# A scan followed by a feed-forward block: order of the first scan, one visit for the outputs of four sequences, accumulator sums on VectorE

## The chip, the cores and the metric

One core of one Trainium2 chip. The metric is the device time of one execution in microseconds (us). All times quoted are of fast runs. The granted TensorE clock is 0.996 to 1.0 in every profiled run.

## The reference

```python
# 4 sequences, 8 heads, 768 positions, head_dim 32, d_state 16, fp32; a is a decay in 0.85..0.95
for c in chunks:                                   # the reference uses chunks of 32 positions
    L = exp(cum_i - cum_j) * causal                # decay between positions of a chunk
    y = (C @ B^T * L) @ x + (C @ state) * exp(cum)
    state = exp(sum(log a)) * state + sum_j decay_j * B_j x_j
x = y as 3072 tokens x 256
h = x @ w_in                                       # 256 -> 2048
out = (h * cos(h)) @ w_out                         # 2048 -> 256
```

## The kernel before

The scan runs in six chunks of 128 positions. While the feed-forward block of chunk c runs in 16 steps, the scan of chunk c+1 is woven into it. A step n: TensorE makes `hp` (128 columns of d_ff times two, for two sequences), ScalarE rounds to whole turns (`k`), VectorE subtracts (`w`), ScalarE takes the cosine, VectorE multiplies (`gT`). Two steps later TensorE multiplies by w_out; from chunk 1 on by a scheme with seven products instead of eight, which needs differences `gd` of gT (GpSimd) and, at the end of each half chunk, sums of seven accumulators. In the first chunk the weights are also rounded for the matrix unit: ScalarE takes `mag` and `last` out of the `words`, GpSimd clips, VectorE joins (two instructions), GpSimd adds (this is called a join below).

The parts that the change touches:

```python
def turn(b, tag=None):                             # transposes of B and C of one sequence, chunk 0
    tp = pair("tp")[:, 0] if tag is None else bank([P, 4 * P], "tp", tag)
    ...
def intra(b):                                      # g = C B^T of 8 heads, then m = g * lam on VectorE
    g = [pair("g") for _ in range(2)]              # a pair is two PSUM banks
    ...
# the first chunk's scan
fill(warm, 2); fill(warm[:, 0:2])                  # warm products: their result is not used
spread_a(0, "h"); turn(0); spread_a(1, "h"); spread_a(2, "o"); spread_a(3, "h")
for b in range(NB): decays0(b)                     # four scans on VectorE
turn(1, "h"); cross(0, "o"); intra(0); turn(2, "h"); cross(2, "o"); intra(1); finish(0, "o")
grade("in", 0, n=2); intra(2); turn(3, "h"); finish(1, "o", 1)
...                                                # decays cut and written to DRAM
join("in", 0); finish(2, "o"); intra(3); grade("in", 1); join("in", 1)

# in step n of the feed-forward block
first(n)                                           # hp, k, w
gate(n)                                            # sine
if not early and n in piece: join(*piece[n])
gated(n)                                           # gT, and gd on GpSimd
second(n - LAG)                                    # products with w_out; after the last of a half: sums
for c, u in pairs(n - 1): intra2(c, u); masked(c, 2 * u)
for c, u in pairs(n - 2): masked(c, 2 * u + 1)
for c, u in pairs(n - 3): finish2(c, u)            # y of two sequences, their part of the state
for c, b, t in halves_at(n): decays(c, b, t)       # half a scan on VectorE, 1.2 to 2.1 us
# TURN = (NF - 5, NF + 3): the pairs' transposes in steps 11 and 19, so two y visits a chunk
# sums of accumulators: four G.tensor_tensor of 128x256 or 128x128
```

Of the kernel before, what the change touches and what calls it, by code (L numbers as in the profile page):

```python
# [25 lines left out]
def kernel(  # L26
# [210 lines left out]
    unit0 = const.tile([P, H, W], FP32, name="unit0")  # L237
# [36 lines left out]
    a0s = const.tile([P, 2, H, W], FP32, name="a0s")  # L274
# [6 lines left out]
    tos = const.tile([P, H, W], FP32, name="tos")  # L281
# [32 lines left out]
    def cross(b, tag):  # L314

        ps = bank([P, H, W], "l_ps", tag)
        PE.matmul(ps, lhsT=fros[:, b:b + 2].rearrange("p b j -> p (b j)"), rhs=tos,
                  start=True, stop=True)
        for t in range(2):
            ACT.copy(out=lam[0, b + t][0:W, 1], in_=ps[t * W:(t + 1) * W])  # L320
            weigh(0, b + t)
# [31 lines left out]
    def turn(b, tag=None):  # L353

        bc = raw[0][0]
        tp = (pair("tp")[:, 0] if tag is None else bank([P, 4 * P], "tp", tag)
              ).rearrange("p (k i) -> p k i", k=4)
        for k in range(2):
            PE.transpose(tp[:, k], bc[:, k, heads(b)].rearrange("p h n -> p (h n)"), ident)

        cT = scan.tile([P, 2, P], FP32, tag="cT", name="cT")
        for t in range(2):
            ACT.activation(cT[:, t], tp[:, 1], AF.Copy, scale=slot[:, t:t + 1])
        bT = scan.tile([P, P], FP32, tag="bT", name="bT")
        ACT.copy(out=bT, in_=tp[:, 0])
        part[0, b] = (bT, cT)

    def intra(b):
# [6 lines left out]
        l = lam.pop((0, b))  # L375
        m = scan.tile([P, 2, H, W], FP32, tag="m", name="m")
# [5 lines left out]
        part[0, b] = m  # L382

# [15 lines left out]
    def turn2(c, u):  # L399
# [12 lines left out]
        rT = scan.tile([P, 2, P], FP32, tag="rT", bufs=1, name="rT")  # L412
# [13 lines left out]
    def masked(c, b):  # L426
# [4 lines left out]
        m = scan.tile([P, H, P], FP32, tag="m", name="m")  # L431
# [7 lines left out]
    def finish2(c, u):  # L439
        (_, ms, rT), xr = part.pop((c, u)), raw[c][1]  # L440
# [3 lines left out]
        for s in range(2):  # L444
            for q in range(4):
                r, p = slice(32 * q, 32 * q + 32), 64 * (q % 2)
                PE.matmul(y[p:p + 64, q // 2, s * P:(s + 1) * P],  # L447
                          lhsT=state[c - 1, u][r, s].rearrange("p t d -> p (t d)"),
                          rhs=rT[r, s], start=(s == 0), stop=False, tile_position=(32 * q, p),
                          skip_group_check=True)  # L450
        for s in range(2):
            for h in range(H):
                q, t = h % 4, h // 4
                PE.matmul(y[32 * q:32 * q + 32, t, s * P:(s + 1) * P], lhsT=xr[:, 2 * u + s, h],  # L454
                          rhs=ms[s][:, h], start=False, stop=True, tile_position=(0, 32 * q),
                          skip_group_check=True)
        if u == 0:
            yT[c] = two.tile([P, 2, TB], FP32, tag="yT", name="yT")
        ACT.copy(out=yT[c][:, :, 2 * u * P:(2 * u + 2) * P], in_=y[:, :, 0:2 * P])
        if c < NC - 1:  # L460
            s_ps = pair("s_ps")[:, 0, 0:4 * D].rearrange("p (s d) -> p s d", s=2)
            for s in range(2):
                sum_up(c, 2 * u + s, s_ps[:, s])
            carry(c, u, s_ps)
# [37 lines left out]
    def first(n):  # L502
# [6 lines left out]
        for e in range(2):  # L509
            fs = slice((2 * j + e) * P, (2 * j + e + 1) * P)  # L510
            for k in range(KT):
                PE.matmul(to_[:, e], lhsT=w_in[:, k, fs], rhs=y[:, k, u],  # L512
                          start=(k == 0), stop=(k == KT - 1), skip_group_check=True)

# [66 lines left out]
    def seven(n):  # L581
# [38 lines left out]
        for dst, a_, b_ in ((sum_[:, 0:2], ps[:, 1:3], ps[:, 0:1]),  # L620
# [3 lines left out]
            G.tensor_tensor(out=dst, in0=a_, in1=b_.to_broadcast([P, dst.shape[1], P]), op=ALU.add)  # L624
# [34 lines left out]
    fill(warm[:, 0:2])  # L659
    spread_a(0, "h")  # L660
    turn(0)
    spread_a(1, "h")
    spread_a(2, "o")
    spread_a(3, "h")
    for b in range(NB):
        decays0(b)
    turn(1, "h")
    cross(0, "o")
    intra(0)
    turn(2, "h")  # L670
    cross(2, "o")
    intra(1)
    finish(0, "o")
    grade("in", 0, n=2)
    intra(2)
    turn(3, "h")
    finish(1, "o", 1)
# [6 lines left out]
    for dst, src in ((a_cut, cut), (a_all, la)):  # L684
# [3 lines left out]
    join("in", 0)  # L688
    finish(2, "o")
    intra(3)  # L690
    grade("in", 1)
    join("in", 1)
# [8 lines left out]
    TURN = (NF - 5, NF + 3)  # L701

    halves_of = {u: [(t - 4 + i, 2 * u + i // 2, i % 2) for i in range(4)]
                 for u, t in enumerate(TURN)}
    ahead = {1: {0: [(4, 0, 0), (6, 0, 1), (8, 1, 0), (9, 1, 1)]}}
# [3 lines left out]
    def first_scan():  # L709

        finish(3, "o")
# [16 lines left out]
    def pairs(n):  # L728

        at = [(1 + (n - t) // NF, u) for u, t in enumerate(TURN) if (n - t) % NF == 0]  # L730
        return [(c, u) for c, u in at if 0 < c < NC]

    def halves_at(n):
        return [(c, b, t) for c in range(1, NC) for u in range(2)
                for m, b, t in ahead.get(c, {}).get(u, halves_of[u]) if m + (c - 1) * NF == n]

    EARLY = 3
    rest_of_loads()
    for n in range(NC * NF + LAG):
        c, f = divmod(n, NF)  # L740
        early = n < EARLY
        if n < NC * NF:
            if f == 0 and c > 0:
                load(c + 2)
            first(n)
            if n == 0:
# [10 lines left out]
            if not early and n in piece:  # L757
                join(*piece[n])
            gated(n)
            if early and n in piece:  # L760
# [10 lines left out]
        for c, u in pairs(n - 2):  # L771
            masked(c, 2 * u + 1)
        for c, u in pairs(n - 3):
            finish2(c, u)
            if u == 1:
                raw.pop(c)
        for c, b, t in halves_at(n):
            decays(c, b, t)
            if t == 1:
                load_a(c + 1, (b,))  # L780
# [34 lines left out]
```

## Time and profile before

| | before |
|---|---|
| time, median of 4 (386.46 of the 3 runs that were known at the prediction) | 386.79 us |
| span of the profiled run | 384.9 us |
| first hp / second hp / first o product | 18.80 / 22.15 / 26.55 us |
| first o to the last matmul | 354.27 us |
| busy: PE, DVE, ACT, POOL | 98, 69, 45, 64% |

The third and fourth rows are read from TensorE's timeline; they cut the span into the front, in which TensorE waits, and the rest, in which it is nearly at its floor. The lines are in the prediction.

### The profile page before, as it was taken

What the parts mean: (1) busy time and instruction counts of PE and PEld (TensorE: products, weight loads), DVE (VectorE), ACT (ScalarE), POOL (GpSimd) and SP (SyncE); (2) the same over time, 40 slices, a digit from 0 to 9 for tenths busy, and PEclk for the clock granted to TensorE, in tenths of its full rate; (3) what the DMA queues carried; (4) which work ended last, traced back from release to release, by engine and by line L of the source; (5) the groups of instructions that cost most, each with busy time, mean ns of one, the idle gap of its engine ahead of it and who ended that gap; (6) DMA issues with size and microseconds to landing.
All of it is one profiled execution on the core that took longest, in us unless ns stands there. A gap on an engine that the chain in (4) does not pass through costs nothing.

```text
span 384.9 us, 7726 instructions
## 1 busy us (share of the span) xinstructions
PE 378.3 (98%) x2982; PEld 331.2 (86%) x2982; DVE 265.9 (69%) x395; ACT 172.9 (45%) x303; POOL 245.4 (64%) x366
## 2 busy tenths in 40 slices
PE   8999999999999999999999999999999999999996
PEld 3578887888899899899899899899899989989995
DVE  7879999678667658657657757756765865863443
ACT  3878566534334334335334434434433433433441
POOL 5757665458859549648648837855955855853751
PEclk9999999999999999999999999999999999999999
DMA  7989899975002951301791301201210000010001
GB/s 83 270 235 266 249 230 137 181 96 151 2 0 63 148 52 57 96 2 54 127 81 55 97 2 56 81 17 43 68 43 1 21 10 0 2 27 3 7 22 27
DMA packets 106371, 30.42 MB, mean 79 GB/s; under 512 B 75520, under 2 KB 102240, under 8 KB 106336
## 3 DMA queue, kind: packets, MB, share of 16 engines
q1 hardware_dynamic: 106176, 29.81, 38.9%
q8 instruction: 23, 0.38, 0.5%
q10 hardware_dynamic: 160, 0.13, 0.1%
q14 instruction: 12, 0.10, 0.1%
HBM read 26.59 MB, written 3.34 MB: 78 GB/s over the span
## 4 chain that ended last, share of the span: by engine, by line
PE 82%; DVE 7%; POOL 3%; ACT 2%; issue 2%; DMA 2%; SPq 1%; ACTq 0%
PE hp L512 37%; PE o L609 32%; PE g L422 3%; PE y L454 3%; DVE mag L209 2%; DVE w L518 2%; DMA xr<-in_x_dram 2%; PE y L447 2%; DVE lam L344 2%; PE o L571 1%; DVE gT L528 1%; PE warm L101 1%; ACT w L523 1%; PE a_ps L298 1%; PE tp L405 1%
## 5 line engine op out<-in xcount | busy, mean ns | idle before, releaser
L512 PE MATMUL hp<-yT,w_in 128*128 128x256 f32 x768 | 184.4, 383 | 0.6 <-POOL w_in L217 0.3
L512 PEld LDWEIGHTS hp<-yT,w_in 128*128 128x128 f32 x768 | 139.2, 190 | 22.7 <-issue 4.5
L553 POOL TENSOR_TENSOR gd<-gT 128x256 f32<-128x256 f32 x79 | 71.9, 911 | 89.5 <-DVE gT L528 86.2
L528 DVE TENSOR_TENSOR gT<-hp,w 128x512 f32<-128x512 f32 x96 | 66.3, 691 | 69.9 <-ACT w L523 60.1
L523 ACT ACTIVATE w<-w,quarter 128x512 f32<-128x512 f32 x96 | 69.3, 722 | 97.2 <-DVE w L518 97.2
L516 ACT ACTIVATE k<-hp 128x512 int32<-128x512 f32 x96 | 57.1, 595 | 90.8 <-PE hp L512 90.7
L518 DVE SCALAR_TENSOR_TENSOR w<-hp,k 128x512 f32<-128x512 f32 x96 | 65.4, 681 | 36.7 <-ACT k L516 36.4
L609 PE MATMUL o<-words,gd 128*128 128x128 f32 x474 | 67.0, 277 | 0.6 <-POOL gd L555 0.6
L609 PEld LDWEIGHTS o<-words,gd 128*128 128x128 f32 x474 | 59.3, 192 | 2.4 <-POOL gd L555 2.2
L344 DVE TENSOR_TENSOR_SCAN lam<-arow,unit 128x512 f32<-128x512 f32 x40 | 55.7, 1394 | 0.0
L609 PEld LDWEIGHTS o<-w_out,gT 128*128 128x128 f32 x316 | 46.9, 191 | 3.6
L609 PE MATMUL o<-w_out,gT 128*128 128x128 f32 x316 | 48.0, 274 | 0.0
L555 POOL TENSOR_TENSOR gd<-gT,gd 128x128 f32<-128x128 f32 x79 | 43.1, 546 | 6.2
L556 POOL TENSOR_TENSOR gd<-gT,gd 128x128 f32<-128x128 f32 x79 | 35.9, 455 | 6.2
L571 PE MATMUL o<-w_out,gT 128*128 128x256 f32 x128 | 30.3, 380 | 0.4 <-POOL w_out L217 0.4
L609 PE MATMUL o<-w_out,gd 128*128 128x128 f32 x158 | 30.6, 275 | 0.0
L609 PE MATMUL o<-words,gT 128*128 128x128 f32 x158 | 30.5, 275 | 0.0
L571 PEld LDWEIGHTS o<-w_out,gT 128*128 128x128 f32 x128 | 24.2, 190 | 4.0 <-POOL w_out L217 0.8
L435 DVE TENSOR_TENSOR m<-g,lam 128x512 f32<-128x512 f32 x40 | 25.6, 681 | 0.0
L624 POOL TENSOR_TENSOR sum<-ps,sum 128x256 f32<-128x256 f32 (+1 forms) x27 | 24.2, 909 | 1.4
L609 PEld LDWEIGHTS o<-w_out,gd 128*128 128x128 f32 x158 | 24.0, 192 | 0.0
L609 PEld LDWEIGHTS o<-words,gT 128*128 128x128 f32 x158 | 24.0, 192 | 0.0
(91 smaller groups left out, 293.9 us busy)
## 6 DMA issues: line engine op xcount, KB each, us to landing
arow<-a_cut SPq DMA_DIRECT2D x20, 512.0 KB
words<-in_moe_w_in_dram SPq DMA_DIRECT2D x8, 512.0 KB
words<-in_moe_w_out_dram SPq DMA_DIRECT2D x8, 512.0 KB
out_dram<-sum SPq DMA_DIRECT2D x18, 128.0 KB
xr<-in_x_dram SPq DMA_DIRECT2D x4, 512.0 KB
along<-a_all SPq DMA_DIRECT2D x20, 64.0 KB
xr<-in_x_dram SPq DMA_DIRECT2D x8, 128.0 KB
bc<-in_B_dram SPq DMA_DIRECT2D x4, 256.0 KB
```

Of the source, the lines that this page charges most:

```text
L344: V.tensor_tensor_scan(out=lam[c, b][:, hs].rearrange("p h i -> p (h i)"), data0=rows_.rearrange("p h i -> p (h i)"), data1=unit.rearrange ...
L435: V.tensor_tensor(out=of[0], in0=g[q][:, :, s * 2 * P:(s + 1) * 2 * P], in1=of[1], op=ALU.mult)
L512: PE.matmul(to_[:, e], lhsT=w_in[:, k, fs], rhs=y[:, k, u], start=(k == 0), stop=(k == KT - 1), skip_group_check=True)
L516: ACT.activation(k, hp[n], AF.Copy, bias=0.25, scale=INV_2PI)
L518: V.scalar_tensor_tensor(out=w, in0=hp[n], scalar=INV_2PI, in1=k, op0=ALU.mult, op1=ALU.subtract)
L523: ACT.activation(cos, cos, AF.Sin, bias=quarter, scale=TWO_PI)
L528: V.tensor_tensor(out=gT[n], in0=hp.pop(n), in1=cos, op=ALU.mult)
L553: G.tensor_tensor(out=d[:, 0:2], in0=g[:, 1:2].to_broadcast([P, 2, P]), in1=g[:, 3::-3], op=ALU.subtract)
L555: G.tensor_tensor(out=d[:, 2], in0=g[:, 0], in1=d[:, 0], op=ALU.subtract)
L556: G.tensor_tensor(out=d[:, 3], in0=g[:, 2], in1=d[:, 2], op=ALU.subtract)
L571: PE.matmul(o[c, u][:, t], lhsT=g[:, 2 * e + t], rhs=w_out[:, 2 * j + e], start=(j == e == t == 0), stop=(j == NJ - 1 and e == 1), skip_gr ...
L609: PE.matmul(at[q], lhsT=a_[q], rhs=w[q], start=(j == 0 and q in starts), stop=(j == NJ - 1), skip_group_check=True)
```

## The change

Its intent: let the first hp, which needs sequences 0 and 1 only, start earlier; enter the small-tile products of y once instead of twice per chunk; relieve GpSimd; and fill VectorE's wait for the sine. The diff, cut to its core:

```diff
-    fill(warm[:, 0:2])
-    ... four scans, then turn, cross, intra of 0 to 3 in turn
+    spread_a(0, "h"); turn(0, ...); spread_a(1, "h"); decays0(0); decays0(1)
+    cross(0, "o"); intra(0); spread_a(2, "o"); turn(1, ...); spread_a(3, "h"); decays0(2); intra(1)
+    grade("in", 0, n=2); finish(0, "o", 1); finish(1, "o", 1); join("in", 0); decays0(3)
+    turn(2, bank([P, 2 * P], "tp", "h")); cross(2, "o")
+    turn(3, intra(2)[0][:, 0, 2 * P:4 * P])       # the fourth's transposes beside the third's g
...
+    first(0, go_on=False); intra(3); turned(0)    # start(): step 0 is taken out of the loop
+    rest = grade(*piece[0], later=True); finish(2, "o"); ...; finish(3, "o"); gate(0)
+    ...; join("in", 1); gated(0); join(*piece[0])
...
+    at_once = (0, 1), {0: 7, 1: 11}, 14           # chunks 2 to 5: transposes in steps 7 and 11, one visit in 14
+    late = [((0,), {0: 11}, ..., 14), ((1,), {1: NF + 2}, ..., NF + 5)]        # chunk 1: two visits
...
+            behind = [masked(c, 2 * u + 1) for pairs(n - 2)] + [halved(...) for halves_at(n)]
+            if n not in piece and behind:
+                behind.pop(0)()                   # ahead of gT
             gated(n)
+            for do in behind: do()
...
-            G.tensor_tensor(out=dst, in0=a_, in1=b_..., op=ALU.add)     # sums of accumulators
+            V.tensor_tensor(out=dst, in0=a_, in1=b_..., op=ALU.add)
```

Three constants moved into the rotating buffers of m, which grew from two to four.

More of the change, by code (lines that the diff above doesn't have):

```diff
@@ L235 @@
     G.tensor_copy(out=unit, in_=ident.unsqueeze(1).to_broadcast([P, HH, P]))
-    unit0 = const.tile([P, H, W], FP32, name="unit0")
+    both = scan.tile([P, 2, H, W], FP32, tag="m", bufs=4, name="both")
+    unit0, tos = both[:, 0], both[:, 1]
     for t in range(2):
@@ L271 @@
                     axis=mybir.AxisListType.XY, op=ALU.add)
-    a0s = const.tile([P, 2, H, W], FP32, name="a0s")
+    a0s = scan.tile([P, 2, H, W], FP32, tag="m", bufs=4, name="a0s")
     halves = a0z.rearrange("p (t i) -> p t i", t=2)
@@ L280 @@
                         in1=mine[:, HH:H].unsqueeze(2).to_broadcast([P, HH, W]), op=ALU.mult)
-    tos = const.tile([P, H, W], FP32, name="tos")
     G.tensor_tensor(out=tos, in0=to.unsqueeze(1).to_broadcast([P, H, W]),
@@ L320, in cross @@
             ACT.copy(out=lam[0, b + t][0:W, 1], in_=ps[t * W:(t + 1) * W])
-            weigh(0, b + t)
     def weigh(c, b):
@@ L351, in decays, with turn @@
         weigh(c, b)
-    def turn(b, tag=None):
+    def turn(b, tp):
         bc = raw[0][0]
-        tp = (pair("tp")[:, 0] if tag is None else bank([P, 4 * P], "tp", tag)
-              ).rearrange("p (k i) -> p k i", k=4)
+        tp = tp.rearrange("p (k i) -> p k i", k=2)
         for k in range(2):
@@ L374, in intra @@
                       rhs=cT[r].rearrange("p t (s i) -> p s t i", s=2), start=True, stop=True)
-        l = lam.pop((0, b))
-        m = scan.tile([P, 2, H, W], FP32, tag="m", name="m")
+        l = lam[0, b]
+        m = scan.tile([P, 2, H, W], FP32, tag="m", bufs=4, name="m")
         for q in range(2):
@@ L382, in intra @@
         part[0, b] = m
+        return g
     def finish(b, tag, fills=0):
@@ L411, in turn2 @@
             ACT.activation(cT[:, :, t], tp[:, :, 1], AF.Copy, scale=slot[:, t:t + 1])
-        rT = scan.tile([P, 2, P], FP32, tag="rT", bufs=1, name="rT")
+        rT = scan.tile([P, 2, P], FP32, tag="rT", name="rT")
         V.tensor_tensor(out=rT, in0=tp[:, :, 1], in1=reach[c, u], op=ALU.mult)
@@ L430, in masked @@
         l = lam.pop((c, b))
-        m = scan.tile([P, H, P], FP32, tag="m", name="m")
+        m = scan.tile([P, H, P], FP32, tag="m", bufs=4, name="m")
         for q in range(2):
@@ L437, in masked, with finish2 @@
         ms.append(m)
-    def finish2(c, u):
-        (_, ms, rT), xr = part.pop((c, u)), raw[c][1]
+    def finish2(c, us):
+        xr = raw[c][1]
+        parts = [(2 * u + s, part[c, u][1][s], part[c, u][2][:, s]) for u in us for s in range(2)]
         y = pair("y")
-        for s in range(2):
+        for i, (b, _, rT) in enumerate(parts):
             for q in range(4):
                 r, p = slice(32 * q, 32 * q + 32), 64 * (q % 2)
-                PE.matmul(y[p:p + 64, q // 2, s * P:(s + 1) * P],
-                          lhsT=state[c - 1, u][r, s].rearrange("p t d -> p (t d)"),
-                          rhs=rT[r, s], start=(s == 0), stop=False, tile_position=(32 * q, p),
+                PE.matmul(y[p:p + 64, q // 2, i * P:(i + 1) * P],
+                          lhsT=state[c - 1, b // 2][r, b % 2].rearrange("p t d -> p (t d)"),
+                          rhs=rT[r], start=(i == 0), stop=False, tile_position=(32 * q, p),
@@ L450, in finish2 @@
                           skip_group_check=True)
-        for s in range(2):
+        for i, (b, m, _) in enumerate(parts):
             for h in range(H):
                 q, t = h % 4, h // 4
-                PE.matmul(y[32 * q:32 * q + 32, t, s * P:(s + 1) * P], lhsT=xr[:, 2 * u + s, h],
-                          rhs=ms[s][:, h], start=False, stop=True, tile_position=(0, 32 * q),
+                PE.matmul(y[32 * q:32 * q + 32, t, i * P:(i + 1) * P], lhsT=xr[:, b, h],
+                          rhs=m[:, h], start=False, stop=True, tile_position=(0, 32 * q),
@@ L456, in finish2 @@
                           skip_group_check=True)
-        if u == 0:
-            yT[c] = two.tile([P, 2, TB], FP32, tag="yT", name="yT")
-        ACT.copy(out=yT[c][:, :, 2 * u * P:(2 * u + 2) * P], in_=y[:, :, 0:2 * P])
+        s_ps = pair("s_ps")[:, 0].rearrange("p (u s d) -> p u s d", u=2, s=2)
+        for i, u in enumerate(us):
+            del part[c, u]
+            if u == 0:
+                yT[c] = two.tile([P, 2, TB], FP32, tag="yT", name="yT")
+            ACT.copy(out=yT[c][:, :, 2 * u * P:(2 * u + 2) * P],
+                     in_=y[:, :, 2 * i * P:(2 * i + 2) * P])
+            for s in range(2 if c < NC - 1 else 0):
+                sum_up(c, 2 * u + s, s_ps[:, u, s, 0:2 * D])
@@ L460, in finish2 @@
         if c < NC - 1:
-            s_ps = pair("s_ps")[:, 0, 0:4 * D].rearrange("p (s d) -> p s d", s=2)
-            for s in range(2):
-                sum_up(c, 2 * u + s, s_ps[:, s])
-            carry(c, u, s_ps)
+            for u in us:
+                carry(c, u, s_ps[:, u, :, 0:2 * D])
     def sum_up(c, b, s_ps):
@@ L500, in turn_of, with first @@
         return (f % 2, f // 2) if c == 0 else divmod(f, NJ)
-    def first(n):
+    def first(n, go_on=True):
         c, f = divmod(n, NF)
@@ L513, in first, with turned @@
                           start=(k == 0), stop=(k == KT - 1), skip_group_check=True)
+        if go_on:
+            turned(n)
+    def turned(n):
         k = ffn.tile([P, TB], I32, tag="k", name="k")
@@ L623, in seven @@
                             (sum_[:, 2:3], ps[:, 6:7], sum_[:, 6:7])):
-            G.tensor_tensor(out=dst, in0=a_, in1=b_.to_broadcast([P, dst.shape[1], P]), op=ALU.add)
+            V.tensor_tensor(out=dst, in0=a_, in1=b_.to_broadcast([P, dst.shape[1], P]), op=ALU.add)
         for s in range(2):
@@ L658 @@
     fill(warm, 2)
-    fill(warm[:, 0:2])
     spread_a(0, "h")
-    turn(0)
+    turn(0, pair("tp")[:, 0, 0:2 * P])
     spread_a(1, "h")
-    spread_a(2, "o")
-    spread_a(3, "h")
-    for b in range(NB):
-        decays0(b)
-    turn(1, "h")
+    decays0(0)
+    decays0(1)
     cross(0, "o")
     intra(0)
-    turn(2, "h")
-    cross(2, "o")
-    intra(1)
-    finish(0, "o")
-    grade("in", 0, n=2)
-    intra(2)
-    turn(3, "h")
-    finish(1, "o", 1)
+    spread_a(2, "o")
+    turn(1, bank([P, 2 * P], "tp", "h"))
+    spread_a(3, "h")
+    decays0(2)
+    intra(1)
+    grade("in", 0, n=2)
+    finish(0, "o", 1)
+    finish(1, "o", 1)
+    join("in", 0)
+    decays0(3)
+    turn(2, bank([P, 2 * P], "tp", "h"))
+    cross(2, "o")
+    turn(3, intra(2)[0][:, 0, 2 * P:4 * P])
     la = const.tile([RB, NU, P], FP32, name="la")
@@ L686 @@
             out=dst.rearrange("(u b) h (c p) -> (b h c) u p", u=NU, p=P), in_=src)
-    join("in", 0)
-    finish(2, "o")
-    intra(3)
-    grade("in", 1)
-    join("in", 1)
+    later = grade("in", 1, later=True)
     piece = {n: ("in", (n + 3) // 2) if n % 2 else ("out", n // 2) for n in range(NF)}
@@ L698 @@
                  NF + 1: [(0, hind), (1, hind)], NF + 3: [(2, hind), (3, hind)]}
-    TURN = (NF - 5, NF + 3)
-    halves_of = {u: [(t - 4 + i, 2 * u + i // 2, i % 2) for i in range(4)]
-                 for u, t in enumerate(TURN)}
-    ahead = {1: {0: [(4, 0, 0), (6, 0, 1), (8, 1, 0), (9, 1, 1)]}}
+    late = [((0,), {0: 11}, [(4, 0, 0), (6, 0, 1), (8, 1, 0), (9, 1, 1)], 14),
+            ((1,), {1: NF + 2}, [(NF - 2 + i, 2 + i // 2, i % 2) for i in range(4)], NF + 5)]
+    at_once = (0, 1), {0: 7, 1: 11}, 14
+    halves_of = {2: [(2, 0, 0), (3, 0, 1), (5, 1, 0), (6, 1, 1), (7, 2, 0), (8, 2, 1), (10, 3, 0),
+                     (11, 3, 1)]}
+    each = [(i - 1, i // 2, i % 2) for i in range(2 * NB)]
+    plan = [(c, NF * (c - 1), *v) for c in range(1, NC) for v in (
+        late if c == 1 else [(*at_once[:2], halves_of.get(c, each), at_once[2])])]
     sums = {}
     def first_scan():
-        finish(3, "o")
         for u in range(2):
@@ L728, in pairs, with halved, ends, start @@
     def pairs(n):
-        at = [(1 + (n - t) // NF, u) for u, t in enumerate(TURN) if (n - t) % NF == 0]
-        return [(c, u) for c, u in at if 0 < c < NC]
+        return [(c, u) for c, at, _, turn_at, _, _ in plan for u in turn_at
+                if at + turn_at[u] == n]
     def halves_at(n):
-        return [(c, b, t) for c in range(1, NC) for u in range(2)
-                for m, b, t in ahead.get(c, {}).get(u, halves_of[u]) if m + (c - 1) * NF == n]
+        return [(c, *h) for c, at, _, _, halves_of, _ in plan for m, *h in halves_of if at + m == n]
+    def halved(c, b, t):
+        decays(c, b, t)
+        if t == 1:
+            load_a(c + 1, (b,))
+    def ends(n):
+        return [(c, us) for c, at, us, _, _, end in plan if at + end == n]
+    def start():
+        first(0, go_on=False)
+        intra(3)
+        turned(0)
+        rest = grade(*piece[0], later=True)
+        finish(2, "o")
+        for b in range(NB):
+            weigh(0, b)
+            del lam[0, b]
+        finish(3, "o")
+        gate(0)
+        for do in (later, rest):
+            if do:
+                do()
+        join("in", 1)
+        gated(0)
+        join(*piece[0])
     EARLY = 3
     rest_of_loads()
+    start()
     for n in range(NC * NF + LAG):
@@ L744 @@
                 load(c + 2)
+            if n == 0:
+                continue
             first(n)
-            if n == 0:
+            if n == 1:
                 first_scan()
@@ L758 @@
                 join(*piece[n])
+            behind = [lambda at=at: halved(*at) for at in halves_at(n)]
+            behind = [lambda at=(c, 2 * u + 1): masked(*at) for c, u in pairs(n - 2)] + behind
+            if n not in piece and behind:
+                behind.pop(0)()
             gated(n)
+            for do in behind:
+                do()
             if early and n in piece:
@@ L770 @@
             masked(c, 2 * u)
-        for c, u in pairs(n - 2):
-            masked(c, 2 * u + 1)
-        for c, u in pairs(n - 3):
-            finish2(c, u)
-            if u == 1:
+        for c, us in ends(n):
+            finish2(c, us)
+            if 1 in us:
                 raw.pop(c)
-        for c, b, t in halves_at(n):
-            decays(c, b, t)
-            if t == 1:
-                load_a(c + 1, (b,))
         for c, u in pairs(n + 1):
```

## The prediction

> **What bounds the kernel now.** I read the page first, then TensorE's timeline from end to end, then the waits, then all engines' timelines for the first 30 us and for one late visit (237 to 258 us).
>
> The page:
>
> ```profile
> PE 378.3 (98%) x2982; PEld 331.2 (86%) x2982; DVE 265.9 (69%) x395; ACT 172.9 (45%) x303; POOL 245.4 (64%) x366
> PE   8999999999999999999999999999999999999996
> ```
>
> TensorE is busy 98% of the span, but its ends are modelled, so I go by start-to-start distances. In TensorE's timeline eight hp instructions start 1.73 us before what follows (216 ns each), and the 14 of a seven-product step take 1.57 us (112 ns each). Multiplying these pitches by the instructions that start after 26.55 us (hp, both forms of o, transposes) gives 318.1 us of the 353.9 us from there to the last matmul. I split the other 35.8 us by looking where a start-to-start distance exceeds the pitch: ten g visits, 1.27 us each, 12.7; ten y visits, 19.8; waits in between, about 4.0 us (3.3 by subtraction; the sum of single waits, with pitches rounded, is 4.0). So from 26.5 us on TensorE is already at its floor but for three things: the switch cost of the small-tile visits, some 4 us of waits, and the front itself, which takes 26.5 us.
>
> One y visit and the step after it, in TensorE's timeline (start, length, instruction):
>
> ```profile
> 103.16 0.39 PE L609 MATMUL o<-words,gT 128*128 128x128 f32 x2
> 103.38 0.39 PE L609 MATMUL o<-w_out,gd 128*128 128x128 f32 x2
> 103.69 0.67 PE L447 MATMUL y<-rT,state 32*64 32x128 f32 x16
> 104.29 1.08 PE L454 MATMUL y<-m,xr 128*32 128x128 f32 x32
> 105.19 0.41 PE L471 MATMUL s_ps<-xr,sc 128*32 128x64 f32 x16
> 105.53 1.99 PE L512 MATMUL hp<-yT,w_in 128*128 128x256 f32 x8
> 107.36 0.61 PE L609 MATMUL o<-w_out,gT 128*128 128x128 f32 x4
> ...
> 108.69 0.39 PE L609 MATMUL o<-w_out,gd 128*128 128x128 f32 x2
> 108.92 1.89 PE L512 MATMUL hp<-yT,w_in 128*128 128x256 f32 x8
> 110.65 0.61 PE L609 MATMUL o<-w_out,gT 128*128 128x128 f32 x4
> ```
>
> Going in, the last two o instructions take 103.69 - 103.38 = 0.31 us, against 0.23 (108.69 to 108.92) where no visit follows: 0.09 lost. Coming out, hp takes 1.83 us instead of 1.73: 0.10 lost. The body is 1.83 us.
>
> Second, a wait that comes once in each half chunk. The timeline of all engines at such a place:
>
> ```profile
> 241.34 0.73 POOL L624 TENSOR_TENSOR sum<-ps 128x256 f32<-128x256 f32 x1
> 242.14 2.87 POOL L624 TENSOR_TENSOR sum<-ps,sum 128x256 f32<-128x256 f32 x3
> 244.97 0.84 POOL L553 TENSOR_TENSOR gd<-gT 128x256 f32<-128x256 f32 x1
> 245.81 0.61 PE L609 MATMUL o<-w_out,gT 128*128 128x128 f32 x4
> 246.40 0.94 PE L609 MATMUL o<-words,gd 128*128 128x128 f32 x6
> ```
>
> GpSimd sums accumulators for 3.7 us while a finished gT waits for its differences. Then the four gT products take 0.59 instead of 0.45 us, and the first gd product runs 0.10 us slower: 0.25 us. I find this at 124.6, 154.9, 185.2, 215.8, 246.1, 276.5, 306.8 and 336.9 us, and once more at 208.7: 2.3 us in all. Larger single ones: 0.83 us at 93.7, behind two weight differences on GpSimd (3.42 us, from 89.73), and 0.48 us at 59.9, where hp waits for a VectorE that has had no idle time since 42 us.
>
> Third, the front:
>
> ```profile
> 6.98 4.80 DVE L308 TENSOR_TENSOR_SCAN lam<-a_ps,unit 128x512 f32<-128x512 f32 x4 [1.22 <-PE a_ps L298]
> 12.08 1.29 DVE L380 TENSOR_TENSOR m<-g,lam 128x512 f32<-128x512 f32 x2 [0.29 <-POOL lam L312]
> 18.80 2.29 PE L512 MATMUL hp<-yT,w_in 128*128 128x256 f32 x8 [0.32 <-POOL w_in L217]
> 22.15 3.98 PE L512 MATMUL hp<-yT,w_in 128*128 128x256 f32 x16
> 26.55 1.99 PE L571 MATMUL o<-w_out,gT 128*128 128x256 f32 x8 [0.42 <-POOL w_out L217]
> ```
>
> All four scans run before the first product with the mask, though the first hp needs two sequences only.
>
> [...] the 128x256 L553 takes 0.73 us alone and 1.51 us at 235.49, beside the scan at 235.26. [...] L638 and L637 show 425 and 293. [...] The first warm products here take 853 ns for 512 columns and the later a_ps pairs 421, so the switch is near 6 us.
>
> **The change part by part.**
>
> *Front.* One warm product goes (2 instructions, 426 ns: 0.85 us). The broadcast decay is ready at 4.33 us, so a_ps may start near 4.8 instead of 5.62[...]: 0.55 us gained at the first scan (6.4 for 6.98). Then two scans instead of four (2 x 1.21) lie ahead of the first mask product, which I put at 9.2 instead of 12.08, once the cross term is copied. From there, adding durations in the new order (m 1.29, ScalarE's mask copies 0.9, grading 4 x 0.43, VectorE's joins 2.1, weight add 0.73): both y copied by 14.5, the first half of w_in at 14.9. TensorE still has the third sequence's transposes, cross, g and the fourth's transposes in front of hp, so hp starts near 16.6, not 18.8. Much of this is given back, since the fourth's mask product and two joins now stand between hp and gT on VectorE: w at 20.3, gT at 22.1 (was 23.3), second hp 21.1 (was 22.15), first w_out piece 25.2, so the first o product at 25.2 instead of 26.55. VectorE, which is nearly gapless from 30 to 60 us, gets ahead by about 1.0. As it would make TensorE wait at 60 us otherwise, I count **1.0 us**. The cut decay rows are written a little later (GpSimd now has joins before them), 18.4 for 17.3; their first reader is at 37.7, so this should hide.
>
> *Four sequences in one y visit.* For chunks 2 to 5 ten visits become six (chunk 1 keeps two). Saved per merge: 0.197 for going in and out, 0.16 where the state products start and change over to the mask products, 0.02 in these, 0.085 at the last group of sums: 0.47 us. Four times: **1.9 us**. Nothing else runs on TensorE meanwhile, so this is all on the path. The next chunk's yT comes earlier than needed (step 14 against 16).
>
> *Sums on VectorE.* GpSimd loses 9 x 3.46 us (L624: 730 + 2 x 1084 + 559); VectorE gains 9 x (3 x 0.425 + 0.29) = 9 x 1.57 = 14 us and goes from 69% to 73%. The nine waits of 0.25 should go: **2.3 us**. The turn of chunk 1's second pair one step earlier puts a g visit (1.27 us) ahead of the product that waits at 93.7: **0.8 us**.
>
> *A half scan or mask product ahead of gT on VectorE.* It fills the 0.86 us in which VectorE waits for the sine, but takes 1.2 to 1.4 us, so gT ends about 0.45 us later. Normally there is slack: hp's bank has about 1.2 us, gd about 2. But the copy of the second accumulator bank follows gT. Before, it ended at 239.23, and that bank's first product came at 238.79 + 6 x 0.112 = 239.46. Now it ends near 239.55 to 239.7, so TensorE waits some 0.2 to 0.3 us with its restart. At seven places where such work stands there: **-2.1 us**. The sums then delay the next w by 1.7 us; where a half scan follows too (three times) gT ends at 7.0 us after its step's start, against the reuse of the bank at 6.6 plus the wait before: **-0.3 us**.
>
> Sum: 1.0 + 1.9 + 2.3 + 0.8 - 2.1 - 0.3 = 3.6 us. From 386.46: 382.9. My sizes for the new waits are the least sure and rather pessimistic, so I say 382.5.
>
> **The rivals.** (a) *VectorE becomes the local bound.* In the step with sums it has 1.37 (w, gT) + 1.39 + 0.68 + 1.57 = 5.0 us of work for a 3.29 us step. For it: the 0.2 us of room at the accumulator bank. Against: the load over a chunk is some 48 us of 60, and the steps after have 0.5 us to spare each. If the waits are twice mine: 385. (b) *The new order removes nearly all waits,* as GpSimd's differences are no longer beside scans (0.73 instead of a mean 0.91 us) and the copy is early enough: all 4 us go, with the merges and 2 us of front: 379. (c) *The front gives nothing,* since a transfer or VectorE's joins set the pace to 60 us: the last visible wait there (59.9) grows by what was won. For it: DMA at 90% and VectorE at 99% in those slices. That leaves 383.9; with (a) 386. (d) *The front gives 2.2 us,* as at its first hp: 381.
>
> **Range and chances.** The merges are firm; front 0 to 2.2 and waits -2 to +3.5 are spread around the centre and independent, which gives 379.8 to 385.0 for 8 in 10. Over 2% faster means below 378.7, which needs everything at its best: 5%. Slower than 394: hardly 1%.
>
> **What would show it.** Right: first hp near 16.6 us and first o near 25.2; y visits of 128 instructions and some 3.4 us in chunks 2 to 4; L624 on VectorE at 425 and 293 ns; no wait of o on gd after sums. For the pessimistic step: o waiting on VectorE's ps copy after half chunks. Wrong: first o at or after 26.5; a larger hp wait near 60 us; VectorE waits over 0.5 us per half chunk.

## The result, and the profile after

The changed kernel takes 384.74 us (median of 4, 384.72 to 385.37) against 386.79 for the kernel before. Ratios are the mean time of one kernel's fast runs over that of the other's of the same rounds, so not quite the ratio of these medians: 0.9953, 95% interval 0.9934 to 0.9971. So the change gains some 1.8 us. 382.5 was predicted, a gain of 4.0. The time lies within the range that was given; the gain is less than half of what was predicted.

From the page of the changed kernel: each engine's busy time; the shares of the chain that ended last; and one group of instructions (line, engine, instruction, count, busy us and mean ns, idle before):

```profile
PE 375.8 (98%) x2982; PEld 329.8 (86%) x2982; DVE 280.0 (73%) x431; ACT 172.3 (45%) x303; POOL 213.4 (56%) x330
...
PE 96%; DVE 2%; issue 0%; POOL 0%; ACT 0%; DVEq 0%; POOLq 0%
...
L563 POOL TENSOR_TENSOR gd<-gT 128x256 f32<-128x256 f32 x79 | 59.6, 754 | 103.3 <-DVE gT L538 74.2
```

TensorE is now 96% of the chain that ended last, and the first instruction of gd takes 754 ns in the mean. Before, it was:

```profile
PE 82%; DVE 7%; POOL 3%; ACT 2%; issue 2%; DMA 2%; SPq 1%; ACTq 0%
...
L553 POOL TENSOR_TENSOR gd<-gT 128x256 f32<-128x256 f32 x79 | 71.9, 911 | 89.5 <-DVE gT L528 86.2
```

**The rest of the span gained, the front lost.** The first o product starts at 28.46 instead of 26.55 us: 1.9 us later. From there to the last matmul it is 350.46 instead of 354.27 us: 3.8 us less. Behind the last matmul the same instructions take 3.95 instead of 3.68 us, which no run explains. The three together are the 1.6 us by which the two profiled spans differ.

The front in the timeline of all engines of the changed kernel:

```profile
17.46 1.29 DVE L379 TENSOR_TENSOR m<-g,lam 128x512 f32<-128x512 f32 x2
...
18.21 0.44 PE L358 MATMUL g<-ident,bc 128*128 128x128 f32 x2 [0.85 <-DVE m L379]
18.49 1.89 PE L518 MATMUL hp<-yT,w_in 128*128 128x256 f32 x8
...
24.70 1.28 POOL L217 TENSOR_TENSOR w_in<-mag,last 128x512 uint32<-128x512 uint32 x1 [0.73 <-ACT last L191]
25.05 1.22 DVE L207 TENSOR_SCALAR mag<-mag 128x512 uint32<-128x512 uint32 x1
27.14 1.27 POOL L217 TENSOR_TENSOR w_out<-mag,last 128x512 uint32<-128x512 uint32 x1 [1.15 <-DVE mag L209]
28.46 1.99 PE L581 MATMUL o<-w_out,gT 128*128 128x256 f32 x8 [0.43 <-POOL w_out L217]
```

Two places stand out. TensorE sat idle for 0.85 us ahead of the fourth sequence's transposes (18.21), until VectorE had made the first half of the third's mask product (17.46). And the mask step L207 of a join took 1.22 us at 25.05, next to a GpSimd add from 24.70 on; where no GpSimd instruction runs beside it, it takes 0.42 us (at 23.93 us in the kernel before).

A y visit of four sequences in TensorE's timeline:

```profile
136.26 0.39 PE L619 MATMUL o<-w_out,gd 128*128 128x128 f32 x2
136.58 1.10 PE L449 MATMUL y<-rT,state 32*64 32x128 f32 x32
137.61 1.95 PE L456 MATMUL y<-m,xr 128*32 128x128 f32 x64
139.38 0.63 PE L477 MATMUL s_ps<-xr,sc 128*32 128x64 f32 x32
139.94 1.99 PE L518 MATMUL hp<-yT,w_in 128*128 128x256 f32 x8
```

The body is 3.36 us (136.58 to 139.94) instead of twice 1.83, and the 0.09 and 0.10 us of going in and out are paid once: 3.56 against 4.05 us.

I took every TensorE start-to-start distance that exceeds the pitch, from the first o on and outside the visits. Before they sum to 3.8 us, after to 2.0: the nine waits of about 0.25 us are gone (eight for gd; the ninth, at 208.70, for the copy of an accumulator bank) and so is the one of 0.83 us at 93.7; the hp wait near 60 us is 0.32 instead of 0.48; and per chunk three new small ones come to 0.41 us. One of them, in the timeline of all engines:

```profile
151.02 0.66 DVE L538 TENSOR_TENSOR gT<-hp,w 128x512 f32<-128x512 f32 x1
151.60 0.67 DVE L629 COPY ps<-o 128x512 f32<-128x512 f32 x1
151.64 0.61 PE L619 MATMUL o<-w_out,gT 128*128 128x128 f32 x4
```

The copy of the second accumulator bank ends at 152.27. TensorE's seventh instruction is the first into that bank and would come at 151.64 + 6 x 0.112 = 152.31. So it is met nearly to the moment: the instruction behind it starts 0.10 us late.

### The profile page after: what moved, and what is told of

It is laid out like the page before. It is cut to its first block, busy times and chain, and to the rows that moved or that the text cites. A ratio compares the mean times of both kernels' runs of the same rounds, so it can differ in the third digit from the quotient of the medians.

```text
span 383.3 us, 7682 instructions
## 1 busy us (share of the span) xinstructions
PE 375.8 (98%) x2982; PEld 329.8 (86%) x2982; DVE 280.0 (73%) x431; ACT 172.3 (45%) x303; POOL 213.4 (56%) x330
## 4 chain that ended last, share of the span: by engine, by line
PE 96%; DVE 2%; issue 0%; POOL 0%; ACT 0%; DVEq 0%; POOLq 0%
PE hp L518 43%; PE o L619 32%; PE o L581 7%; PE g L422 3%; PE y L456 2%; PE y L449 1%; PE a_ps L299 1%; PE tp L405 1%; PE warm L101 1%; PE g L372 1%; PE o L658 0%; PE s_ps L477 0%; DVE mag L207 0%; DVE m L379 0%; POOL w_out L217 0%
## 5 line engine op out<-in xcount | busy, mean ns | idle before, releaser
L563 POOL TENSOR_TENSOR gd<-gT 128x256 f32<-128x256 f32 x79 | 59.6, 754 | 103.3 <-DVE gT L538 74.2
L538 DVE TENSOR_TENSOR gT<-hp,w 128x512 f32<-128x512 f32 x96 | 65.1, 678 | 32.2 <-ACT w L533 29.6
L566 POOL TENSOR_TENSOR gd<-gT,gd 128x128 f32<-128x128 f32 x79 | 46.1, 583 | 6.2
L565 POOL TENSOR_TENSOR gd<-gT,gd 128x128 f32<-128x128 f32 x79 | 42.8, 541 | 6.2
L327 POOL TENSOR_TENSOR sc<-bc,lam 128x128 f32<-128x128 f32 x20 | 8.4, 429 | 14.1 <-DVE lam L344 7.2
```

The costliest lines, as they stand in the source:

```text
L538: V.tensor_tensor(out=gT[n], in0=hp.pop(n), in1=cos, op=ALU.mult)
L563: G.tensor_tensor(out=d[:, 0:2], in0=g[:, 1:2].to_broadcast([P, 2, P]), in1=g[:, 3::-3], op=ALU.subtract)
L565: G.tensor_tensor(out=d[:, 2], in0=g[:, 0], in1=d[:, 0], op=ALU.subtract)
L566: G.tensor_tensor(out=d[:, 3], in0=g[:, 2], in1=d[:, 2], op=ALU.subtract)
```

## The experiments

Each was run beside the kernel before, in five rounds, and gave correct results. Times are medians; the kernel before had 386.0 to 386.5 in these calls.

| run | edit | time, us | ratio to before | first o | first o to last |
|---|---|---|---|---|---|
| e0 | changed kernel again | 385.05 | 0.9954 | 28.60 | 350.42 |
| e1 | fourth's transposes in an own bank | 383.76 | 0.9931 | 26.41 | 350.46 |
| e2 | old front | 383.42 | 0.9923 | 26.91 | 350.62 |
| e3 | new front alone | 387.51 | 1.0036 | 27.56 | 354.06 |
| e4 | sums on GpSimd | 388.49 | 1.0049 | 28.57 | 354.64 |
| e5 | half scans between gT and copy | 393.01 | 1.0166 | 28.47 | 358.59 |
| e6 | half scans at the end of the step | 390.45 | 1.0104 | 27.70 | 356.71 |
| e7 | e6 and e4 | 386.92 | 1.0013 | 27.81 | 353.09 |
| e8 | e2 less one warm product | 382.28 | 0.9890 | 25.41 | 350.57 |
| e9 | e1 with an earlier join | 385.86 | 0.9993 | 28.96 | 350.31 |
| e10 | two y visits per chunk | 386.65 | 1.0003 | 27.69 | 352.34 |
| e11 | e1 with the mask step moved | 383.50 | 0.9931 | 27.37 | 350.44 |

The intervals of the ratios are about 0.0013 to either side (0.5 us). The last column repeats within 0.2 us where the steady part is the same. The column before it does not: with the same front, e0, e3, e5, e6, e7 and e10 spread over 1.0 us. The reason shows in TensorE's timelines. The changed kernel's first broadcast products:

```profile
4.78 1.98 PE L299 MATMUL a_ps<-a0s,those 128*64 128x512 f32 x4
```

The same four instructions in e1, whose program is the same up to there:

```profile
4.58 1.08 PE L299 MATMUL a_ps<-a0s,those 128*64 128x512 f32 x4
```

In the first they take 1.98 us, in the second 1.08, which is also what the changed kernel's next four take (at 7.13 us). So the first scan starts at 6.82 or at 5.74 us, by the run; what decides this, no run shows. Differences in single traces of up to 1.1 us in the front are therefore not to be explained by an edit; I measure the front from the first scan, or from the first mask product, instead. From first scan to first o the kernel before, e2 and e8 have 19.56 to 19.57 us, and the eight traces of the changed front with the shared bank 21.53 to 21.78.

### e0: the changed kernel again

No edit.

> The changed kernel itself once more, unedited, so that the next three are compared with it on the same chip and in the same rounds. Expected: 0.994 to 0.997 of the kernel before. Also open: how far the front differs from profile to profile, since the first scan started at 6.82 us in two runs and at 5.74 in one.

0.9954, as in the first measurement (0.9953). First scan at 6.82 again.

### Which part loses: e2 and e3

e2 is the changed kernel with `fill(warm[:, 0:2])`, the order of scans, `turn`, `weigh` and step 0 of the kernel before; e3 is the kernel before with the new ones:

```diff
 e2 (against the changed kernel)             e3 (against the changed kernel)
-    start()                                 -            behind.pop(0)() ...          # ahead of gT
+    fill(warm[:, 0:2])                      +            behind, after second(n - LAG) and finish2
+    ... the old order, turn(3, bank "h")    -    V.tensor_tensor(... sums)
                                             +    G.tensor_tensor(... sums)
                                             +    plan: transposes in 11 and 19, two visits
```

> Edit: the changed kernel with the front of the kernel before (order of the first chunk's scan, second warm product, transposes in banks of hp); the merged y visits, the half scans ahead of gT and the sums on VectorE stay. Theory (front costs 1.9 us, the rest gains 3.8): first o product at 26.5 us, time 386.8 - 3.8 = 383.0, faster than both kernels. Rival (VectorE, already without idle time to 60 us, gives the front's difference back whatever the order): 384.7 as the changed kernel.

> Edit: the kernel before with the new front alone (two scans first, fourth's transposes in the third's g bank, one warm product less); turns, visits, order of half scans and GpSimd's sums are as before. Theory (the front is the part that loses): 0.8 to 1.8 us slower than the kernel before, and first o 21.6 us after the first scan instead of 19.6. Rival (the front gains[...]): 0.5 to 1 us faster than the kernel before.

e2 has 383.42 us, 0.9923 against e0's 0.9954: the front costs 1.2 us. The expectation of 383.0 took 1.9 us from one trace, the one whose first broadcast products took 1.98 us. e3, the front alone, is 1.4 us slower than the kernel before (1.0036), with 21.54 us from first scan to first o. The two agree within their intervals. The rest of the change, in e2, gains 3.0 us.

### The shared bank: e1

```diff
-    turn(3, intra(2)[0][:, 0, 2 * P:4 * P])
+    intra(2)
+    turn(3, bank([P, 2 * P], "tp", "o"))
```

> Edit: the changed kernel, but the fourth sequence's transposes go to a PSUM bank of their own (the o pair) instead of the free half of a bank of the third's g. Theory (the new front loses because these transposes, and so the first hp, wait until VectorE has read g out of that bank): transposes right behind the third's g near 17.4 us, first hp near 17.7 instead of 18.5, the fourth's mask product near 19.7 instead of 21.2, first o product near 26.8 instead of 28.5, time about 1.5 us below the changed kernel (383.2). Rival (VectorE's and ScalarE's joins and copies set the pace of the front, the bank does not): first hp earlier, but first o stays within 0.4 us of 28.5 and the time at 384.5 or more.

```profile
16.12 0.44 PE L358 MATMUL tp<-ident,bc 128*128 128x128 f32 x2
16.29 1.29 DVE L379 TENSOR_TENSOR m<-g,lam 128x512 f32<-128x512 f32 x2
...
16.39 1.94 PE L518 MATMUL hp<-yT,w_in 128*128 128x256 f32 x8
...
22.66 1.28 POOL L217 TENSOR_TENSOR w_in<-mag,last 128x512 uint32<-128x512 uint32 x1 [0.17 <-ACT last L191]
22.74 1.48 DVE L207 TENSOR_SCALAR mag<-mag 128x512 uint32<-128x512 uint32 x1
...
24.25 0.69 DVE L209 SCALAR_TENSOR_TENSOR mag<-words,mag 128x512 uint32<-128x512 uint32 x1
25.09 1.27 POOL L217 TENSOR_TENSOR w_out<-mag,last 128x512 uint32<-128x512 uint32 x1 [1.16 <-DVE mag L209]
```

The transposes now come right behind g and ahead of the mask product. The ratio goes from 0.9954 to 0.9931: 0.9 us. In the traces, first mask product to first o goes from 18.36 to 17.47 us: 0.88; the eight traces of the changed front with the shared bank have 18.33 to 18.36, so this distance repeats within 0.03. The theory holds, with a smaller size than the 1.5 us expected. The columns that the transposes wrote were not those that VectorE read, yet in the changed kernel TensorE waited 0.85 us with them until VectorE's product was made. What an access without this wait would do, no run shows; in e1, with an own bank, the wait is gone, which is worth the 0.9 us.

From first scan to first o, e1 still takes 20.68 us against 19.56 of the old front.

### The rest of the front: e9 and e11

In e1 the lines above show the mask step at 1.48 us beside GpSimd's add, with the rest of the join and the first o product (26.41) right behind. From the start of the first gT (22.14) to first o it is 4.27 us, in the kernel before, where the mask step takes 0.42, 3.22 us. e9 moves the whole join of the second w_in piece ahead of the fourth's mask product; e11 moves only the mask step of the following join (w_out) ahead of the first gT, where the add has not begun:

```diff
 e9 (against e1)                             e11 (against e1)
     first(0, go_on=False)                        join("in", 1)
+    later()                                 +    shift(*piece[0])          # L207 alone
+    join("in", 1)                                gated(0)
     intra(3)                                -    join(*piece[0])
...                                          +    join(*piece[0], shifted=True)
-    later(), join("in", 1) before gated(0)
```

> Edit: the run with the fourth's transposes in a bank of their own, and the second piece of w_in is joined before the fourth's mask product instead of between w and gT of the first step. In that run VectorE's mask step L207 of the next join took 1.48 us instead of 0.42, beside GpSimd's add L217. Theory (the rest of the front's loss, 1.1 us, is this collision on the way to the first w_out piece): L207 there at 0.4 to 0.5 us, first o product 19.6 to 20.1 us after the first scan instead of 20.7, time 0.6 to 1.0 us below that run's 383.8. Rival (the join only moves, and puts the fourth's y and the second hp back by as much): second hp later, first o within 0.3 us of 20.7 after the first scan.

> Edit: the run with the fourth's transposes in a bank of their own; VectorE's mask step L207 of the first w_out piece is put before the first gT, that is before GpSimd's add L217 of w_in begins, instead of after it, beside that add. Nothing else moves (the run before this one moved a whole join and lost 2 us elsewhere). If the collision (L207 1.48 us instead of 0.42) lies on the path to the first o product: L207 at 0.4 to 0.5 us, first o 20.2 to 20.5 us after the first scan instead of 20.7. If it is hidden: still 20.7. The time should move by less [...], 383.2 to 384.0, so the distance in the trace decides.

e9 missed its theory and came out worse than its rival: L207 took 0.43 us, but it waited until 19.94 for a clip on GpSimd that stands behind the cut of the decays. The fourth's mask product came later, and the ratio rose by 0.0062 (2.4 us; in the traces 22.73 us from first scan to first o instead of 20.68). e11 in the timeline of all engines:

```profile
23.80 0.41 DVE L203 TENSOR_SCALAR mag<-mag 128x512 uint32<-128x512 uint32 x1
24.07 1.29 POOL L223 TENSOR_TENSOR w_in<-mag,last 128x512 uint32<-128x512 uint32 x1 [0.74 <-ACT last L191]
...
24.73 1.17 DVE L215 SCALAR_TENSOR_TENSOR mag<-words,mag 128x512 uint32<-128x512 uint32 x1
```

The mask step takes 0.41 us, and now the second step of the join (L215, 0.7 us elsewhere) runs into the add. From first scan to first o it is 20.55, 0.13 less than e1, which alone would not reach the expected range; but in e11's run the second scan came 0.25 us later after the first, ahead of the place of the edit. From the first mask product it is 17.09 instead of 17.47: 0.38 less. So the collision is on the path, in part. The time, 0.9931, is as e1's and says nothing. From gT to first o it is now 3.24 us, but the moved step stands in front of gT (0.41 us) and L215 pays 0.48 us of the collision. So e11 does not take the collision away, it moves it. Of the 1.1 us by which the new order is slower than the old even with its own bank, 0.4 are shown to be this collision. The other 0.7 may be what is left of it, as the 1.05 us between gT and first o in e1 suggest; no run removes it entirely without losing elsewhere, so this is not shown.

### Sums on VectorE and work ahead of gT: e4, e5, e6, e7

```diff
 e4:  -V.tensor_tensor(... sums)  +G.tensor_tensor(... sums)
 e5:  -if n not in piece and behind:  +if False:            # all of behind follows gT at once
 e6:  -behind.pop(0)(); gated(n); behind  +gated(n); ... second(n - LAG) ... finish2 ...; behind
 e7:  e6 and e4
```

> Edit: the changed kernel with the sums of accumulators back on GpSimd, nothing else. Theory (of the waits that went, the nine of 0.25 us came from these sums): waits of o for gd come back after each half chunk, 1.5 to 2.5 us slower than the changed kernel, 386.2 to 387.2. Rival (the differences got quicker because scans no longer run beside them, so GpSimd has room for the sums): within 0.4 us of the changed kernel.

> Edit: the changed kernel, but no half scan or mask product stands ahead of gT on VectorE: all of them follow it. The prediction's term (work ahead of gT delays the copy of the accumulator bank and costs 2.1 us): 1 to 2 us faster than the changed kernel. Rival (what it fills is idle time, and without it the w of the next step comes late and GpSimd's differences run beside the scans again): 0.3 to 1.5 us slower than the changed kernel, L563 at 0.9 us mean instead of 0.75.

> Edit: the changed kernel, but half scans and mask products stand where the kernel before had them, at the end of the step, after the products and sums of accumulators, instead of ahead of gT. This undoes that part properly; the run before it put them between gT and the copy of the accumulator bank. Prediction's term (work ahead of gT costs 2.1 + 0.3 us): 1 to 2.5 us faster than the changed kernel. Rival (it lets w of the next step and GpSimd's differences come in time): 0.5 to 4 us slower than the changed kernel, with o waiting for gd after half chunks.

> Edit: as the run above, and the sums of accumulators back on GpSimd: of the steady part only the new turns and the visit for four sequences stay. If merging gives its 1.97 us by itself and the nine waits of 0.25 us stay, and the front costs 1.2 us: 0.2 to 1 us below the kernel before, some 1 us slower than the changed kernel. If turns at 7 and 11 themselves crowd GpSimd or VectorE: 1 us or more above the kernel before.

e5 is not the undoing that I meant: the kernel before has the half scans behind the copy of the accumulators, e5 puts them between gT and that copy, and TensorE waits about 1.0 us per half chunk for the copy. e6 is the proper one. With e0, e4, e6 and e7 there are all four combinations, as ratios to the kernel before:

| | sums on VectorE | sums on GpSimd |
|---|---|---|
| work ahead of gT | 0.9954 | 1.0049 |
| work at the end of the step | 1.0104 | 1.0013 |

Each alone makes the kernel 1.4 us (0.0036) or 3.5 us (0.0091) slower than neither; together they gain 2.3 us (0.0059). Against the changed kernel, e4, e5 and e6 are 3.7, 8.2 and 5.8 us slower: each goes the way of one of its expectations, but further than expected, and in e6 it is not o that waits for gd. e7, 0.5 us above the kernel before, lies between its two. What happens in e4, ahead alone:

```profile
155.69 2.86 POOL L634 TENSOR_TENSOR sum<-ps,sum 128x256 f32<-128x256 f32 x3
158.89 0.72 POOL L563 TENSOR_TENSOR gd<-gT 128x256 f32<-128x256 f32 x1
160.19 0.94 PE L619 MATMUL o<-words,gd 128*128 128x128 f32 x6 [0.92 <-POOL gd L565]
```

The half scan ahead of gT, in the step with the sums, puts their start to 1.25 us after the next hp (154.89 and 153.64), in e7 0.90 (154.89 and 153.99); a product for the scan's state (L327, 0.41 us) falls between them and gd; and TensorE waits 1.2 us for gd, whose gT was ready 3.6 us before. Such waits for gd stand behind four half chunks in e4 and, of about 0.3 us, behind three in e7. So they are not the 0.25 us behind nearly every half chunk that the kernel before had. In e6, sums on VectorE alone:

```profile
155.81 1.21 DVE L344 TENSOR_TENSOR_SCAN lam<-arow,unit 128x512 f32<-128x512 f32 x1
156.94 0.66 DVE L528 SCALAR_TENSOR_TENSOR w<-hp,k 128x512 f32<-128x512 f32 x1
158.46 0.69 DVE L538 TENSOR_TENSOR gT<-hp,w 128x512 f32<-128x512 f32 x1 [0.86 <-ACT w L533]
```

The copy, the sums (ended 155.89) and a half scan stand in one row between two steps, so w comes at 156.94, gT ends at 159.15, and hp, whose bank it frees, starts at 159.30 after 0.95 us of waiting. In the changed kernel the half scan has moved into the time before gT, in which VectorE waits for the sine, and only copy and sums stand before w: it starts 0.83 us after the next hp has begun (154.15 and 153.32), in e6 1.81 us after (156.94 and 155.13).

### The visits: e10

```diff
-        late if c == 1 else [(*at_once[:2], halves_of.get(c, each), at_once[2])])]
+        late if c == 1 else [((0,), {0: 7}, halves_of.get(c, each)[:4], 10),
+                             ((1,), {1: 11}, halves_of.get(c, each)[4:], 14)])]
```

> Edit: the changed kernel, but chunks 2 to 5 finish their two pairs in two visits (steps 10 and 14) as before. If the visit's switch costs are all that merging saves: 4 x 0.49 = 2.0 us slower than the changed kernel, 387.0. Rival (the extra visit gives VectorE and GpSimd 2 us more in step 10, so waits shrink): under 1 us slower.

386.65 us, 1.0003 against 0.9954: 1.9 us, as expected. In the trace, first o to last grows by 1.9 us.

### A faster version: e8

```diff
 e2's front
-    fill(warm[:, 0:2])
```

> Edit: the old front with the new steady part (383.4 us, the fastest so far), without its second warm product. Theory (the warm product holds the first broadcast product back by 0.85 us[...]): 0.2 to 0.6 us faster, 383.0. Rival ([...] less warm work means only longer cold products): within 0.2 us.

382.28 us (382.17 to 382.41), 0.9890: faster than both kernels and 1.3 us faster than e2, more than twice what was expected. The first broadcast product starts at 4.69 instead of 5.63, and in this trace the first four take 1.08 us, in e2's 1.64, so nothing was lost again. How often that is so, one trace does not say. So dropping the warm product, a part of the change, is a gain; what loses in the front is the order. Against e8, which lacks that product too, the new order with the shared bank (e0) costs 2.5 us (0.0064) and with an own bank (e1) 1.6 us (0.0041).

## Why the prediction was wrong

**The front: the step that failed.** The prediction counted a gain of 1.0 us ("hp starts near 16.6, not 18.8", "the first o product at 25.2 instead of 26.55"). Timed, the front loses 1.2 to 1.4 us. Its own steps against the trace of the changed kernel:

| step | predicted | measured | late by |
|---|---|---|---|
| first scan | 6.4 | 6.82 | 0.4 |
| first mask product | 9.2 | 10.11 | 0.9 |
| both y copied | 14.5 | 15.78 | 1.3 |
| first half of w_in | 14.9 | 16.05 | 1.15 |
| first hp | 16.6 | 18.49 | 1.9 |
| w of step 0 | 20.3 | 22.43 | 2.1 |
| second hp | 21.1 | 23.48 | 2.4 |
| first o | 25.2 | 28.46 | 3.3 |

The lateness grows at three places. Up to the first mask product it is the slow first products of TensorE (the first scan at 6.82 us here and at 5.74 in e1, the same program part: 1.08 us) and short waits of the chain itself. At the first hp it is the bank: the prediction put the fourth's transposes right behind the third's g and did not ask who else uses that bank; e1 gives 0.9 us, and with the own bank first mask product to first hp takes 7.45 us, where the prediction has 7.4. Between w and first o it is the join that collides with GpSimd's add: the prediction had read gd at 1.51 us beside a scan and 0.73 alone, and then added up "VectorE's joins" at their lone durations; e11 shows 0.4 us of it on the path, and about 0.7 us of the front's loss stays open. It expected late decay writes to hide, and they did: no wait for them shows.

Rival (c), "the front gives nothing", was nearest, but for another reason: the hp wait near 60 us did not grow (0.32 us), so neither transfers nor VectorE's work up to 60 us took the gain back. It was never there.

**The visits: right.** 0.47 us per merge were predicted and 0.49 measured; 1.9 in all, e10 gives 1.9. What costs the 0.10 us coming out is not shown: in the kernel before, the first o product (1.83 us from 26.55 us on instead of 1.73) and the restart after a wait at 94.53 (0.77 instead of 0.67) lose as much, with no visit before them.

**The nine waits and the one at 93.7: right in size.** 2.3 and 0.8 us, all gone in the trace. One of the nine was misread: at 208.70 TensorE did not wait for gd but for the copy of the second accumulator bank, which ended at 208.94; its product starts at 208.99. And the sums were not free to move by themselves: without the work ahead of gT they cost 3.5 us. The prediction called that work the price of the change (-2.1 us). With the sums on VectorE it is what pays for them (5.8 us, e0 against e6); only with the sums on GpSimd does it cost, 1.4 us. So its sign was wrong for the kernel as changed, which did not show in the total, because both came together.

**New waits: the places right, the size too large.** 2.4 us were predicted, 1.4 measured: seven waits for the copy, 1.0 us together (2.1 predicted), and three for the bank that gT frees, 0.4 us (0.3 predicted). The copy ends 2.36 us after the hp that starts its step (149.91 and 152.27), against 2.17 before (237.06 and 239.23), so 0.2 us later; 0.3 to 0.5 was assumed. gT and the copy are 0.66 us each and overlap by 0.08. The sums take 2.0 us per half chunk instead of 1.57 (18.3 us in all): three of the four run beside GpSimd's differences, at 0.64, 0.56 and 0.56 us, where the prediction took 0.425 from an instruction beside which nothing runs.

Summed in the trace: predicted from first o on 1.9 + 2.3 + 0.8 - 2.4 = 2.6 us, measured 3.8 (3.0 timed in e2, whose trace has 3.65 there, less 0.36 of a later first o and 0.28 behind the last matmul); front +1.0 predicted, -1.9 measured (-1.2 timed). The two errors partly cancel, and it is luck that the time still fell into the range.

One reading in the prediction does not come out of its trace, without weight for the result: from 26.55 us to the last matmul it is 354.27, not 353.9 us, so that 3.7 us of waits are left by subtraction, not 3.3. The switch of TensorE's rate "near 6 us" does come out of it: the second warm product's instruction at 4.63 takes 426 ns for 256 columns, per column as long as 853 for 512; the first pair of broadcast products, at 5.62, takes 0.69 us until the next, the pairs from 8.11 us on 0.43.

## What to carry to other kernels

A free corner of a PSUM bank was not a free buffer here: the writer waited 0.85 us for the reader of the bank's other columns, and as it stood ahead of the first hp on TensorE, that product came late too (8.38 us after the first mask product, 7.45 with an own bank). Judge two parts of a change in all four combinations before calling one of them the price: here each alone lost 1.4 to 3.5 us and both together gained 2.3. And when adding durations in a new order, ask for each SBUF instruction of VectorE what GpSimd does at that moment: here the mask step took 0.42 us alone and 1.22 and 1.48 beside a GpSimd add of 1.28 us, the second step of the join 0.69 alone and 1.17 beside one of 1.29. And measure a front from an event after TensorE's slow first products, which moved the first scan by 1.08 us between two runs of the same program part.
